# Token-major layout for the routing search's comparison tiles and list masks, fed by pairs of equal elements

## The chip, the cores and the metric

The kernel runs on one core of one Trainium2 chip. The metric is the device time of one execution in microseconds (us), the median of several runs. Engine names are those of the profile: PE is TensorE's matmuls, PEld its weight loads, DVE is VectorE, ACT is ScalarE, POOL is GpSimd, SP is the engine that issues most transfers.

## The reference

Three stages follow one another: a chunked attention, a two-layer MLP, and a mixture of 8 experts whose assignment is greedy over all (token, expert) scores. The change is in the third stage's assignment.

```python
def _moe2_ref(x, w_gate, w1, w2):          # x: 3072 x 512
    E = w_gate.shape[1]                    # 8 experts
    cap = N // E                           # 384 tokens each
    flat = (x @ w_gate).flatten()
    order = np.argsort(-flat)
    for idx in order:                      # best score first
        tok, e = idx // E, idx % E
        if assigned[tok] >= 0 or counts[e] >= cap:
            continue
        assigned[tok] = e
        counts[e] += 1
    ...
    for e in range(E):
        h = np.maximum(x[assigned == e] @ w1[e], 0.0)
        out[assigned == e] = h @ w2[e]
```

## The kernel before, in words

Attention and the MLP fill the first 670 us or so. Every large product there and in the experts is computed as three float32 products of high and low parts, and TensorE is what these stages run on. The experts follow. For each expert p the kernel finds which expert fills up next and with which tokens (`search`), makes the list of its 384 tokens (`tail`), gathers their rows, and runs the two products of that expert (`gemm1` at L610, `gemm2` at L633). Seven searches are run; the eighth expert takes what is left. A search for expert p+1 runs while the products of expert p are computed, so its small matmuls stand between large ones in TensorE's queue, and its vector work stands between the conversions of weights (L591, L593) on ACT and DVE.

A search looks for a score threshold, five or six bits of a 24-bit key at a time, in six levels (`LEVELS`). At each level `differ` forms the key's difference for the 24 tokens that each of the 128 partitions holds (`d`, 128 x 24), `compare` (L300) compares every one of them with 32 or 64 thresholds (`cm`, 24 x 32 = 768 or 24 x 64 = 1536 elements per partition, bfloat16), and `count` (L312) multiplies `cm` with the one-hot matrix `oh` of the tokens' best experts, so that each threshold's number of tokens per expert comes out. A matmul of `count` has 128 columns of `cm` as its weights: 32 thresholds of 4 tokens, in which case 6 matmuls with 32 moving columns make a level (four levels of a search), or 64 thresholds of 2 tokens, in which case 12 matmuls with 16 moving columns do (two levels). `less`, `threshold` and `base` (L318, L326, L329, L333) turn the counts into the next `d`. So a search is a chain that goes back and forth between DVE and PE.

For the list, `slots` computes each token's place (0 to 31, and 1 to 12), `places` and `parts` (L441, L448, L450) turn the two numbers into masks `A` and `rh`, and `tokens` (L459) multiplies them in 6 matmuls with 48 moving columns.

In all of these tiles the token column is innermost or nearly so: `cm` is stored as [group of tokens, threshold, token in the group], with 6 or 12 tokens in a group. A matmul takes one token of each group, so that the 128 weights lie 6 or 12 elements, 12 or 24 bytes, apart. `A` has the same layout with 6; the moving operand `rh` is also read in steps. The constants `i32`, `top` and `thr` are spread out over the tokens so that DVE reads whole rows of them.

The order of all instructions is written out when the program is built, by a planner (`Plan`) with fixed costs. Every engine then runs its own list in that order and waits for semaphores. Between the MLP's end and the first expert's products, TensorE runs a backlog of the MLP's second product (L1035) and then dummy matmuls (L663).

Of the kernel before, what the change touches and what calls it, by code (L numbers as in the profile page):

```python
# [170 lines left out]
UPPER = 4  # L171
PACK = 4


def routing_consts(nc, pool, jp, NTILE, E):
    V, G = nc.vector, nc.gpsimd
    c = {}

    def iota(name, cols, dt=FT, **kw):
        x = c[name] = pool.tile([128, cols], dt, name=name)  # L180
        G.iota(x, **({} if dt == I32 else dict(allow_small_or_imprecise_dtypes=True)), **kw)
        return x

    def fill(name, shape, dt, value):
        x = c[name] = pool.tile(shape, dt, name=name)
        V.memset(x, value)

    c["i32"] = pool.tile([128, 32, NTILE], F16, name="i32")
    G.iota(c["i32"], pattern=[[1, 32], [0, NTILE]], base=0, channel_multiplier=0, allow_small_or_imprecise_dtypes=True)
    top = pool.tile([128, 64, NTILE // 2], F16, name="top")  # L190
    G.iota(top, pattern=[[1, 64], [0, NTILE // 2]], base=1, channel_multiplier=0, allow_small_or_imprecise_dtypes=True)
    c["thr"] = []
    for n, (step, R) in enumerate(LEVELS):
        c["thr"].append(pool.tile([128, R, NTILE * R // 128], BF, name=f"thr{n}"))
        V.tensor_scalar(c["thr"][n], top[:, :R, :NTILE * R // 128], step, None, op0=OP.mult)
# [4 lines left out]
    iota("token", NTILE, F16, pattern=[[128, NTILE]], base=-HALF, channel_multiplier=1)  # L200
# [12 lines left out]


def phase2(tc, P, C, ident, L, x2d, we, out, ps_h, ps_o, ps_y, pools, lready, xready, open_pools, open_experts, room, roomy, before):
# [6 lines left out]
    nc = tc.nc  # L222
    NTILE, E = L.shape[1], L.shape[2]
# [52 lines left out]
    def differ(p, n):  # L276

        r = R[p]
        v = r["d"] = rt([128, NTILE], BF, "d")
        zero = C[0]["zero"]  # L280
        if n < UPPER:
            V.scalar_tensor_tensor(v, r["km"][:, n], r["pb"][:, 0:1] if n else 0.0, zero,
                                   op0=OP.subtract, op1=OP.subtract)
        else:
            if n == UPPER:
                r["no"] = rt([128, NTILE], FT, "no")
                V.scalar_tensor_tensor(r["no"], r["key"][2], r["pb"][:, 0:1], C[0]["far"],
                                       op0=OP.subtract, op1=OP.mult)
            V.scalar_tensor_tensor(v, r["km"][:, n], r["pb"][:, 1:2] if n > UPPER else 0.0, r["no"],
                                   op0=OP.subtract, op1=OP.subtract)  # L290
# [12 lines left out]

    def count(p, n):

        r = R[p]
        T, K, W = shape(n)
        r["pc"] = pools["ps_r"].tile([128, K * E], FT, name="pc")
        oh = r["oh"].rearrange("p (a b) e -> p a b e", b=W)
        cm = r["cm"].rearrange("p a t b -> p (a t) b")  # L310
        for j in range(W):
            nc.tensor.matmul(r["pc"], cm[:, :, j], oh[:, :, j, :], start=(j == 0), stop=(j == W - 1))  # L312

    def less(p, n, m):
        r = R[p]
# [110 lines left out]
    def slots(p):  # L426

        r = R[p]
        b = rt([128, NTILE], FT, "sb")
        a = rt([128, NTILE], I16, "sl")  # L430
        V.tensor_scalar(b, r["fx"][:, :NTILE], r["ps"], 32.0, op0=OP.add, op1=OP.add)
        V.tensor_tensor(a, b, r["F"], op=OP.mult)
        s = r["sl"] = rt([128, 2, NTILE], I16, "sp")
        V.tensor_scalar(s[:, 0], a, 31, None, op0=OP.bitwise_and)
        V.tensor_scalar(s[:, 1], a, 5, None, op0=OP.logical_shift_right)

    def places(p):
        c, r = C[0], R[p]
        W = NTILE // PACK
        r["A"] = rt([128, PACK, 32, W], F16, "A")  # L440
        V.tensor_tensor(r["A"], c["i32"][:, :, :W][:, None].to_broadcast([128, PACK, 32, W]),  # L441
                        r["sl"][:, 0].rearrange("p (a b) -> p a b", a=PACK)[:, :, None, :]
                        .to_broadcast([128, PACK, 32, W]), op=OP.is_equal)

    def parts(p):
        c, r = C[0], R[p]
        oc = rt([128, 12, NTILE], F16, "oc")
        V.tensor_tensor(oc, c["i32"][:, 1:13], r["sl"][:, None, 1].to_broadcast([128, 12, NTILE]), op=OP.is_equal)  # L448
        r["rh"] = rt([128, 12, NTILE], F16, "rh")
        V.tensor_tensor(r["rh"], oc, c["token"][:, None, :].to_broadcast([128, 12, NTILE]), op=OP.mult)  # L450

    def tokens(p):

        r = R[p]
        W = NTILE // PACK
        r["px"] = pools["ps_t"].tile([128, PACK, TT, 4], FT, name="pt")
        A, rh = r["A"], r["rh"].rearrange("p n (a b) -> p a n b", a=PACK)
# [105 lines left out]
    W, REG = {}, {}  # L563
# [97 lines left out]
    b, o = ps_o[0].take(), before  # L661
# [5 lines left out]
    for p in range(E):  # L667
# [7 lines left out]
        for f in range(NF + 2):  # L675
# [3 lines left out]
            s = NF * p + f - 2  # L679
# [9 lines left out]
def kernel(ctx, tc, q, k, v, w, w_gate_t, we, out):  # L689
# [513 lines left out]
    def expert_pools():  # L1203
# [67 lines left out]
```

## Time and profile before

| | |
|---|---|
| median of 3 runs | 1005.46 us (1004.71 to 1007.41) |
| time of the profiled execution | 1007.31 us |
| span of the profiled execution | 1005.3 us |
| PE busy | 983.8 us, 98% of the span |
| DVE busy | 768.5 us, 76% |
| ACT busy | 444.8 us, 44% |
| POOL busy | 131.6 us, 13% |
| mean granted TensorE clock | 0.996 of full speed |

Span is from the first to the last instruction; the profiled execution's own time is 2.0 us more. A matmul's recorded duration contains its way through the array, and records of neighbouring matmuls overlap, so what a matmul costs in a dense stretch is the distance from its start to the next one's start.

### The profile page before, as it was taken

The page shows a single profiled execution, that of the slowest core. Times are in us where ns is not written, and L with a number is a line of the kernel's source. Part 1 is how long each engine was busy: PE and PEld are TensorE (multiplying, and loading weights), DVE is VectorE, ACT ScalarE, POOL GpSimd, SP SyncE. Part 2 cuts the span into 40 slices and gives each one's busy share as a digit, 9 for nine tenths or more (in the row PEclk, how much of TensorE's full clock was granted, in tenths as well). Part 3 has the DMA queues.
Part 4 walks back from the last instruction along what each step waited for, and adds up shares of the span by engine and source line. Part 5 has one row for each costly group of instructions (what it writes and reads, how often), then busy time and mean ns, then how long its engine had stood idle before and what let it go on. Part 6 is the DMA issues. An engine that isn't in the chain of part 4 may idle for free.

```text
span 1005.3 us, 17330 instructions
## 1 busy us (share of the span) xinstructions
PE 983.8 (98%) x6068; PEld 856.7 (85%) x6068; DVE 768.5 (76%) x2573; ACT 444.8 (44%) x1187; POOL 131.6 (13%) x145
## 2 busy tenths in 40 slices
PE   8899999999999999999999999999999999999997
PEld 7778888888888888988888889778888888888996
DVE  6899798698698599699689494578887888875720
ACT  7777634444444443444444324023524334334521
POOL 0578521000000000000000000000121112111211
PEclk9999999999999999999999999999999999999999
DMA  7567510121011011110110000034542534526600
GB/s 260 196 212 236 191 58 29 31 74 44 29 61 58 30 61 50 38 62 30 58 62 11 1 1 31 12 119 133 174 162 96 199 113 141 170 71 202 227 32 32
DMA packets 36328, 95.50 MB, mean 95 GB/s; under 512 B 4369, under 2 KB 8465, under 8 KB 36113
## 3 DMA queue, kind: packets, MB, share of 16 engines
q1 hardware_dynamic: 32256, 81.54, 24.4%
q0 software_dynamic: 3840, 12.59, 3.7%
q8 instruction: 48, 0.79, 0.3%
q14 instruction: 40, 0.32, 0.1%
q10 hardware_dynamic: 144, 0.26, 0.1%
HBM read 81.79 MB, written 12.58 MB: 94 GB/s over the span
## 4 chain that ended last, share of the span: by engine, by line
PE 84%; DVE 7%; issue 4%; POOL 2%; ACT 1%; DMA 1%; POOLq 0%; DVEq 0%; ACTq 0%
PE po L1035 24%; PE ph L942 23%; PE ph L610 13%; PE po L633 12%; PE pa L824 3%; PE pa L894 2%; PE pc L312 2%; DVE junk L1065 2%; PE po L1090 2%; PE pa L867 2%; DVE wa L921 1%; DVE wp L919 1%; PE pt L479 1%; DVE wp L918 1%; DVE gs L951 1%
## 5 line engine op out<-in xcount | busy, mean ns | idle before, releaser
L1065 DVE CUSTOM_DVE_ANT_0 junk<-x,wgb 128x512 bf16<-128x512 f32 x296 | 207.5, 701 | 5.9 <-DMA wgb<-in_w_gate_t_dram 0.9
L950 ACT ACTIVATE gs<-ph 128x384 f32<-128x384 f32 x128 | 62.6, 489 | 196.9 <-PE ph L942 188.2
L1035 PE MATMUL po<-wouth,gh 128*128 128x512 f32 x336 | 136.4, 406 | 0.0
L1035 PE MATMUL po<-woutl,gh 128*128 128x512 f32 x336 | 133.7, 398 | 1.6 <-POOL woutl L926 1.6
L951 DVE TENSOR_TENSOR gs<-ph,gs 128x384 f32<-128x384 f32 x128 | 70.9, 554 | 82.2 <-ACT gs L950 81.8
L1035 PE MATMUL po<-wouth,gl 128*128 128x512 f32 x336 | 132.0, 395 | 0.7 <-POOL gl L953 0.7
L833 ACT ACTIVATE X<-X,st 96x128 f32<-96x128 f32 x248 | 96.9, 392 | 47.5 <-DVE st L828 47.3
L942 PE MATMUL ph<-x1h,winh 128*128 128x384 f32 x512 | 111.6, 339 | 0.4 <-DVE gs L951 0.4
L942 PE MATMUL ph<-x1h,winl 128*128 128x384 f32 x512 | 110.7, 337 | 0.2 <-POOL winl L926 0.2
L942 PE MATMUL ph<-x1l,winh 128*128 128x384 f32 x512 | 110.3, 336 | 0.0
L616 ACT ACTIVATE egh<-ph 128x384 fp32r<-128x384 f32 x64 | 31.4, 491 | 157.4 <-PE ph L610 148.0
L942 PEld LDWEIGHTS ph<-x1h,winh 128*128 128x128 f32 x512 | 91.6, 188 | 10.2 <-DVE gs L951 0.8
L942 PEld LDWEIGHTS ph<-x1h,winl 128*128 128x128 f32 x512 | 92.3, 188 | 1.4 <-POOL winl L926 0.5
L942 PEld LDWEIGHTS ph<-x1l,winh 128*128 128x128 f32 x512 | 91.1, 189 | 0.3
L1035 PEld LDWEIGHTS po<-wouth,gl 128*128 128x128 f32 x336 | 63.1, 188 | 15.4 <-POOL gl L953 1.9
L1035 PEld LDWEIGHTS po<-wouth,gh 128*128 128x128 f32 x336 | 63.1, 188 | 13.8
L1035 PEld LDWEIGHTS po<-woutl,gh 128*128 128x128 f32 x336 | 63.2, 188 | 13.1 <-POOL woutl L926 2.9
L952 ACT ACTIVATE gh<-gs 128x384 fp32r<-128x384 f32 x112 | 58.7, 524 | 34.4 <-DVE gs L951 34.0
L617 DVE SCALAR_TENSOR_TENSOR egl<-ph,egh 128x384 fp32r<-128x384 f32 x64 | 35.2, 551 | 45.1 <-ACT egh L616 45.0
L828 DVE CUSTOM_DVE_ANT_0 X<-pa,masks 96x128 f32<-96x128 f32 x232 | 56.3, 281 | 4.8 <-PE pa L824 4.8
L953 DVE TENSOR_TENSOR gl<-gs,gh 128x384 fp32r<-128x384 f32 x88 | 48.5, 551 | 10.7 <-ACT gh L952 10.6
L1150 POOL IOTA ij<- 128x128 int32 x1 | 0.2, 235 | 425.8 <-DVE L L1065 425.8
(245 smaller groups left out, 1938.9 us busy)
## 6 DMA issues: line engine op xcount, KB each, us to landing
west<-in_we_dram SPq DMA_DIRECT2D x56, 512.0 KB, 4.5
wst<-in_w_dram SPq DMA_DIRECT2D x32, 512.0 KB, 4.3
vt<-in_v_dram SPq DMA_DIRECT2D x30, 256.0 KB, 2.6
kt<-in_k_dram SPq DMA_DIRECT2D x30, 256.0 KB, 3.5
qt<-in_q_dram SPq DMA_DIRECT2D x31, 192.0 KB, 3.1
x2d<-x SPq DMA_DIRECT2D x21, 256.0 KB, 2.2
x<-in_we_dram SPq DMA_DIRECT2D x16, 256.0 KB, 2.8
wgb<-in_w_gate_t_dram SPq DMA_DIRECT2D x1, 2048.0 KB, 7.0
```

The lines of the kernel that those rows point to most:

```text
L610: nc.tensor.matmul(ph.t[:, :TB], w[a].t[:, k * 128:(k + 1) * 128], xs[x].t[:, k, :], start=(n == 0), stop=(n == 3 * KD - 1))
L617: b = P.op(("V", 0.47), lambda: V.scalar_tensor_tensor(gl.t, ph.t[:, :TB], 0.0, gh.t.bitcast(FT), op0=OP.max, op1=OP.subtract), [a], [ph, ...
L633: nc.tensor.matmul(ACC[p][i].t, l.t[:, 128 * i:128 * i + 128], w[a].t[:, 512:1024], start=(f == 0 and n == 0), stop=(f == NF - 1 and n == 2))
L828: V.tensor_tensor_reduce(out=X.t[:, h, :], in0=ps[h % 2].t[:QB, h // 2 * 128:h // 2 * 128 + 128], in1=masks[:, var, :], scale=-scale, scal ...
L833: S.activation(X.t[:, h, :], X.t[:, h, :], AF.Exp, bias=st.t[:, 0, h:h + 1], scale=-1.0, accum_out=st.t[:, 2, h:h + 1])
L942: nc.tensor.matmul(ph.t[:, :TB], win[wt][:, f, kk * 128:(kk + 1) * 128], xt.t[:, kk, :], start=(n == 0 and kk == 0), stop=(n == 2 and kk = ...
L950: o = P.op(("S", 0.37), lambda: S.activation(t.t, ph.t[:, :TB], AF.Copy, scale=0.01), [o], [ph, t], key=k)
L951: o = P.op(("V", 0.47), lambda: V.tensor_tensor(t.t, ph.t[:, :TB], t.t, op=OP.max), [o], [ph, t], key=k)
L952: x = P.op(("S", 0.42), lambda: S.activation(gh(), t.t, AF.Copy), [o, gd], [t, *gb], key=k)
L953: y = P.op({"V": 0.47} if j > 1 else {"V": 0.47, "G": 0.96} if j else {"G": 0.96}, lambda e=V if j > 1 else G: e.tensor_tensor(gl(), t.t, ...
L1035: nc.tensor.matmul(acc.t, lt()[:, sl], wout[wt][:, f, :], start=(f == 0 and n == 0), stop=(n == 2 and (f == NF - 1 or s == S6 - 1)), skip_ ...
L1065: V.tensor_tensor_reduce(out=pools["wgb"].tile([128, DM], BF, name="junk"), in0=x, in1=WGB[0][:, e, :], scale=1.0, scalar=0.0, op0=OP.mult ...
```

## The change

The token column becomes the outermost dimension. `cm` is [24 tokens, thresholds], `A` is [24, 32], `rh` is [24, 12]. The weights of each matmul in `count` and `tokens` are then 128 neighbouring elements, and the moving operands are neighbouring elements as well. For the comparison, a new helper `pairs` reads the row of thresholds two by two, and the token's value from a tile in which each value stands twice (`d` is 128 x 24 x 2, the list's places are 128 x 2 x 24 x 2, `token` is 128 x 48), so that the innermost dimension of all three operands has two neighbouring 16-bit elements. The constants shrink: `i32` from 768 elements per partition to 32, `top` from 768 to 64, `thr` from 192 or 768 to 32 or 64.

The planner's costs are not touched, and no instruction is added, removed or moved: PE, DVE, ACT, POOL and SP have 3532, 2492, 657, 141 and 290 rows in their written-out order before and after, and row by row they are the same instructions on the same tiles, but for the sizes of `d`, `sp`, `thr`, `i32`, `top` and `token`.

```diff
-    c["i32"] = pool.tile([128, 32, NTILE], F16, name="i32")
-    G.iota(c["i32"], pattern=[[1, 32], [0, NTILE]], base=0, channel_multiplier=0, allow_small_or_imprecise_dtypes=True)
-    top = pool.tile([128, 64, NTILE // 2], F16, name="top")
...
+    iota("i32", 32, F16, pattern=[[1, 32]], base=0, channel_multiplier=0)
+    top = iota("top", 64, F16, pattern=[[1, 64]], base=1, channel_multiplier=0)
...
-        c["thr"].append(pool.tile([128, R, NTILE * R // 128], BF, name=f"thr{n}"))
+        c["thr"].append(pool.tile([128, R], BF, name=f"thr{n}"))
...
     def differ(p, n):
-        v = r["d"] = rt([128, NTILE], BF, "d")
+        v = r["d"] = rt([128, NTILE, 2], BF, "d")
+        two = lambda x: x[:, :, None].to_broadcast([128, NTILE, 2])
...
+    def pairs(out, row, column, op):
+
+        n = row.shape[1] // 2
+        V.tensor_tensor(out.rearrange("p c (t u) -> p c t u", u=2),
+                        row.rearrange("p (t u) -> p t u", u=2)[:, None].to_broadcast([128, NTILE, n, 2]),
+                        column[:, :, None, :].to_broadcast([128, NTILE, n, 2]), op=op)
 
     def compare(p, n):
         c, r = C[0], R[p]
         T, K, W = shape(n)
-        cm = r["cm"] = rt([128, K, T, W], BF, f"cm{T}")
-        V.tensor_tensor(cm, c["thr"][n][:, None].to_broadcast([128, K, T, W]),
-                        r["d"].rearrange("p (a b) -> p a b", a=K)[:, :, None, :].to_broadcast([128, K, T, W]),
-                        op=OP.is_le)
+        cm = r["cm"] = rt([128, NTILE, T], BF, f"cm{T}")
+        pairs(cm, c["thr"][n], r["d"], OP.is_le)
 
     def count(p, n):
...
-        oh = r["oh"].rearrange("p (a b) e -> p a b e", b=W)
-        cm = r["cm"].rearrange("p a t b -> p (a t) b")
         for j in range(W):
-            nc.tensor.matmul(r["pc"], cm[:, :, j], oh[:, :, j, :], start=(j == 0), stop=(j == W - 1))
+            c = slice(j * K, j * K + K)
+            nc.tensor.matmul(r["pc"], r["cm"][:, c, :].rearrange("p a t -> p (a t)"),
+                             r["oh"][:, c, :].rearrange("p a e -> p (a e)"), start=(j == 0), stop=(j == W - 1))
...
-        s = r["sl"] = rt([128, 2, NTILE], I16, "sp")
+        s = r["sl"] = rt([128, 2, NTILE, 2], I16, "sp")
...
     def places(p):
-        r["A"] = rt([128, PACK, 32, W], F16, "A")
...
+        r["A"] = rt([128, NTILE, 32], F16, "A")
+        pairs(r["A"], c["i32"], r["sl"][:, 0], OP.is_equal)
 
     def parts(p):
-        oc = rt([128, 12, NTILE], F16, "oc")
...
+        oc = rt([128, NTILE, 12], F16, "oc")
+        pairs(oc, c["i32"][:, 1:13], r["sl"][:, 1], OP.is_equal)
...
     def tokens(p):
...
-            nc.tensor.matmul(r["px"], A[:, :, :, j].rearrange("p a m -> p (a m)"), rh[:, :, :, j],
-                             start=(j == 0), stop=(j == W - 1))
+            c = slice(j * PACK, j * PACK + PACK)
+            nc.tensor.matmul(r["px"], r["A"][:, c, :].rearrange("p a m -> p (a m)"),
+                             r["rh"][:, c, :].rearrange("p a n -> p (a n)"), start=(j == 0), stop=(j == W - 1))
```

## Rows read from the trace of the kernel before

**Rows 1.** The page: busy time and share of the span, TensorE.

```profile
PE 983.8 (98%) x6068; PEld 856.7 (85%) x6068; DVE 768.5 (76%) x2573; ACT 444.8 (44%) x1187; POOL 131.6 (13%) x145
```

**Rows 2.** Busy us by stretch: its length, then PE, PEld, DVE, ACT, POOL.

```profile
671.50:686.60 15.10, 11.80 (x104) 10.19 (x103) 11.83 (x37) 7.51 (x13) 3.56 (x3) 1.00 0.68 220
705.00:905.00 200.00, 200.00 (x1192) 169.06 (x1191) 167.40 (x610) 78.04 (x148) 33.73 (x44) 1.00 0.41 139
```

**Rows 3.** All that PE waited for from 620 us on: total us, times, longest.

```profile
PE pc L312 <- DVE cm L300: 1.5, 3, 0.7
PE ph L610 <- ACT xth L482: 1.1, 1, 1.1
PE pb L333 <- DVE fl L329: 1.0, 3, 0.6
PE ph L479 <- DMA xg<-x2d,idx: 0.8, 1, 0.8
```

**Rows 4.** Timeline, PE alone: three runs of small matmuls and what follows; start, duration.

```profile
637.77 0.45 PE L312 MATMUL pc<-oh,cm 128*128 128x32 bf16 x6
638.07 0.48 PE L1035 MATMUL po<-wouth,winl 128*128 128x512 f32 x1
...
653.95 0.87 PE L312 MATMUL pc<-oh,cm 128*128 128x16 bf16 x12
654.68 0.48 PE L1035 MATMUL po<-woutl,winh 128*128 128x512 f32 x1
...
665.15 0.72 PE L459 MATMUL pt<-rh,A 128*128 128x48 f16 x6
665.64 0.48 PE L1035 MATMUL po<-woutl,winh 128*128 128x512 f32 x1
```

**Rows 5.** The same, windows that end after the first two matmuls of a run.

```profile
637.77 0.27 PE L312 MATMUL pc<-oh,cm 128*128 128x32 bf16 x2
...
653.95 0.28 PE L312 MATMUL pc<-oh,cm 128*128 128x16 bf16 x2
```

**Rows 6.** The same: one matmul on packed bf16 weights; two with weights loaded before.

```profile
662.05 0.18 PE L424 MATMUL pt<-fx,tri 128*128 128x1 bf16 x1
662.09 0.47 PE L1035 MATMUL po<-wouth,winh 128*128 128x512 f32 x1
...
720.50 0.23 PE L312 MATMUL pc<-oh,cm 128*128 128x32 bf16 x2
```

**Rows 7.** Loads, matmuls by line, ns min/median/max; L312 in two runs, L424.

```profile
L312 PEld LDWEIGHTS <-cm x6: 125/144/148, 637.8 to 638.0; 128*128 128x128 bf16 x6
L312 PE MATMUL pc<-oh,cm x6: 197/198/219, 637.8 to 638.0; 128*128 128x32 bf16 x6
...
L312 PEld LDWEIGHTS <-cm x12: 140/166/168, 653.9 to 654.6; 128*128 128x128 bf16 x12
...
L424 PEld LDWEIGHTS <-tri x8: 95/96/98, 662.0 to 930.3; 128*128 128x128 bf16 x8
```

**Rows 8.** Groups by line and form, DVE: busy us, mean ns, idle before.

```profile
L593 DVE TENSOR_TENSOR wl<-west,wh 128x512 fp32r<-128x512 f32 x64 | 41.8, 683 | 0.0
...
L300 DVE TENSOR_TENSOR cm<-thr,d 128x768 bf16<-128x768 bf16 x28 | 15.5, 554 | 0.6
...
L300 DVE TENSOR_TENSOR cm<-thr,d 128x1536 bf16<-128x1536 bf16 x14 | 13.4, 955 | 0.3
...
L272 DVE TENSOR_TENSOR oh<-rev,be 128x192 bf16<-128x192 f32 x7 | 2.5, 358 | 0.2
```

**Rows 9.** Timeline where the routing constants are made.

```profile
598.99 0.93 POOL L189 IOTA i<- 128x768 f16 x1
...
599.87 1.08 POOL L191 IOTA top<- 128x768 f16 x1
...
601.00 0.15 POOL L181 IOTA token<- 128x24 f16 x1
...
603.19 0.96 PE L942 MATMUL ph<-x1h,winh 128*128 128x384 f32 x4 [0.35 <-DVE gs L951]
```

More of the change, by code (lines that the diff above doesn't have):

```diff
@@ L186, in fill @@
         V.memset(x, value)
-    c["i32"] = pool.tile([128, 32, NTILE], F16, name="i32")
-    G.iota(c["i32"], pattern=[[1, 32], [0, NTILE]], base=0, channel_multiplier=0, allow_small_or_imprecise_dtypes=True)
-    top = pool.tile([128, 64, NTILE // 2], F16, name="top")
-    G.iota(top, pattern=[[1, 64], [0, NTILE // 2]], base=1, channel_multiplier=0, allow_small_or_imprecise_dtypes=True)
+    iota("i32", 32, F16, pattern=[[1, 32]], base=0, channel_multiplier=0)
+    top = iota("top", 64, F16, pattern=[[1, 64]], base=1, channel_multiplier=0)
     c["thr"] = []
     for n, (step, R) in enumerate(LEVELS):
-        c["thr"].append(pool.tile([128, R, NTILE * R // 128], BF, name=f"thr{n}"))
-        V.tensor_scalar(c["thr"][n], top[:, :R, :NTILE * R // 128], step, None, op0=OP.mult)
+        c["thr"].append(pool.tile([128, R], BF, name=f"thr{n}"))
+        V.tensor_scalar(c["thr"][n], top[:, :R], step, None, op0=OP.mult)
     c["mask"] = pool.tile([128, len(LEVELS), NTILE], I32, name="mask")
@@ L199, in routing_consts @@
     iota("rev", E, pattern=[[-1, E]], base=E, channel_multiplier=0)
-    iota("token", NTILE, F16, pattern=[[128, NTILE]], base=-HALF, channel_multiplier=1)
+    iota("token", 2 * NTILE, F16, pattern=[[128, NTILE], [0, 2]], base=-HALF, channel_multiplier=1)
     fill("cap", [128, E], FT, float(NTILE * 128 // E))
@@ L278, in differ @@
         r = R[p]
-        v = r["d"] = rt([128, NTILE], BF, "d")
-        zero = C[0]["zero"]
+        v = r["d"] = rt([128, NTILE, 2], BF, "d")
+        two = lambda x: x[:, :, None].to_broadcast([128, NTILE, 2])
+        zero = two(C[0]["zero"])
         if n < UPPER:
-            V.scalar_tensor_tensor(v, r["km"][:, n], r["pb"][:, 0:1] if n else 0.0, zero,
+            V.scalar_tensor_tensor(v, two(r["km"][:, n]), r["pb"][:, 0:1] if n else 0.0, zero,
                                    op0=OP.subtract, op1=OP.subtract)
@@ L288, in differ @@
                                        op0=OP.subtract, op1=OP.mult)
-            V.scalar_tensor_tensor(v, r["km"][:, n], r["pb"][:, 1:2] if n > UPPER else 0.0, r["no"],
+            V.scalar_tensor_tensor(v, two(r["km"][:, n]), r["pb"][:, 1:2] if n > UPPER else 0.0, two(r["no"]),
                                    op0=OP.subtract, op1=OP.subtract)
@@ L432, in slots @@
         V.tensor_tensor(a, b, r["F"], op=OP.mult)
-        s = r["sl"] = rt([128, 2, NTILE], I16, "sp")
-        V.tensor_scalar(s[:, 0], a, 31, None, op0=OP.bitwise_and)
-        V.tensor_scalar(s[:, 1], a, 5, None, op0=OP.logical_shift_right)
+        s = r["sl"] = rt([128, 2, NTILE, 2], I16, "sp")
+        two = a[:, :, None].to_broadcast([128, NTILE, 2])
+        V.tensor_scalar(s[:, 0], two, 31, None, op0=OP.bitwise_and)
+        V.tensor_scalar(s[:, 1], two, 5, None, op0=OP.logical_shift_right)
     def places(p):
         c, r = C[0], R[p]
-        W = NTILE // PACK
-        r["A"] = rt([128, PACK, 32, W], F16, "A")
-        V.tensor_tensor(r["A"], c["i32"][:, :, :W][:, None].to_broadcast([128, PACK, 32, W]),
-                        r["sl"][:, 0].rearrange("p (a b) -> p a b", a=PACK)[:, :, None, :]
-                        .to_broadcast([128, PACK, 32, W]), op=OP.is_equal)
+        r["A"] = rt([128, NTILE, 32], F16, "A")
+        pairs(r["A"], c["i32"], r["sl"][:, 0], OP.is_equal)
     def parts(p):
         c, r = C[0], R[p]
-        oc = rt([128, 12, NTILE], F16, "oc")
-        V.tensor_tensor(oc, c["i32"][:, 1:13], r["sl"][:, None, 1].to_broadcast([128, 12, NTILE]), op=OP.is_equal)
-        r["rh"] = rt([128, 12, NTILE], F16, "rh")
-        V.tensor_tensor(r["rh"], oc, c["token"][:, None, :].to_broadcast([128, 12, NTILE]), op=OP.mult)
+        oc = rt([128, NTILE, 12], F16, "oc")
+        pairs(oc, c["i32"][:, 1:13], r["sl"][:, 1], OP.is_equal)
+        r["rh"] = rt([128, NTILE, 12], F16, "rh")
+        V.tensor_tensor(r["rh"].rearrange("p c (t u) -> p c t u", u=2), oc.rearrange("p c (t u) -> p c t u", u=2),
+                        c["token"].rearrange("p (c u) -> p c u", u=2)[:, :, None, :].to_broadcast([128, NTILE, 6, 2]),
+                        op=OP.mult)
     def tokens(p):
@@ L456, in tokens @@
         r["px"] = pools["ps_t"].tile([128, PACK, TT, 4], FT, name="pt")
-        A, rh = r["A"], r["rh"].rearrange("p n (a b) -> p a n b", a=PACK)
         for j in range(W):
-            nc.tensor.matmul(r["px"], A[:, :, :, j].rearrange("p a m -> p (a m)"), rh[:, :, :, j],
-                             start=(j == 0), stop=(j == W - 1))
+            c = slice(j * PACK, j * PACK + PACK)
+            nc.tensor.matmul(r["px"], r["A"][:, c, :].rearrange("p a m -> p (a m)"),
+                             r["rh"][:, c, :].rearrange("p a n -> p (a n)"), start=(j == 0), stop=(j == W - 1))
     def indices(p):
```

## The prediction

> **What bounds the kernel now.** I read the page first, for the engine that is never free: PE is busy for 98% of the span [rows 1]. Since that is an average, I then looked at stretches [rows 2]. From 705 to 905 us, where five of the seven searches lie between the experts' products, PE is busy for all of the 200.00 us and DVE for 167.40. In the start-up of the experts, 671.5 to 686.6 us, PE is busy for 11.80 of 15.10 us, dummies among them, and DVE for 11.83; there expert 0's weights and rows are awaited. The list of waits comes third: from 620 us to the end PE waited only 4.4 us in four rows [rows 3]. Behind 690 us, therefore, a microsecond taken out of PE's own queue is a microsecond of the span, and one taken out of DVE's is worth nothing until PE waits for it. So the question is what the small matmuls cost PE, and that is read from starts, not from recorded durations.
>
> **What a run of small matmuls costs now.** A run of 6 in `count` goes from 637.77 to the next large matmul at 638.07, 0.30 us; a run of 12 from 653.95 to 654.68, 0.73 us; a run of 6 in `tokens` from 665.15 to 665.64, 0.49 us [rows 4]. How the steps lie: two matmuls of the first run take 0.27 us together and one within a run lasts 0.198, so that the second starts 0.07 us after the first; in the run of 12 it is 0.28 less 0.20, 0.08 us [rows 5, 7]. The other steps are (0.30 - 0.07) / 5 = 0.046 us and (0.73 - 0.08) / 11 = 0.059 us. So 16 moving columns step more slowly than 32: it is not the moving operand that sets the step but the weights, which lie 24 bytes apart there and 12 here. The weight loads say the same: the first of a run, which waits behind nothing, takes 125 ns at 12 bytes and 140 ns at 24, but 95 to 98 ns for `tri`, whose 128 x 128 bf16 weights are packed [rows 7]. In `tokens` the weights lie 12 bytes apart too, and the mean step is 0.49 / 6 = 0.08 us; what is slower there is the moving operand, 48 elements that each lie apart from the next.
>
> **What it costs after.** No row shows packed weights in a run, so I bound the step. From below: where two sets of weights had been loaded ahead, the second matmul started 0.23 - 0.20 = 0.03 us after the first [rows 6]; nothing in these rows goes faster with 32 columns. From above: the step that the 12-byte weights have already, 0.046. Between: the lone matmul on `tri` gives way to the next after 0.04 us [rows 6], and the first step of a strided run is longer than its later ones by 0.02 (0.07 against 0.046, 0.08 against 0.059), because later loads overlap the matmul ahead. A lone packed matmul with 16 to 48 columns would take some 0.05, the later ones 0.02 less. I take 0.05 for the first and 0.03 for each other one, for all three kinds, since it is what both ways of reckoning give.
>
> - `count` with 32 thresholds: 0.05 + 5 x 0.03 = 0.20 in place of 0.30 us, 28 runs: 2.8 us.
> - `count` with 64: 0.05 + 11 x 0.03 = 0.38 in place of 0.73 us, 14 runs: 4.9 us.
> - `tokens`: 0.20 in place of 0.49 us, 8 runs: 2.3 us.
>
> Together 10.0 us of PE's queue. The large matmul behind each run still waits for its own weights; that part is not in these figures and stays.
>
> What of it is not on the path: in the start-up stretch three runs of the first kind and one of the second (0.65 us) lie where PE has time to spare; DVE's chain there does wait for them, so I take off 0.5. Search 0 lies beside the backlog. A shorter run lets the backlog end earlier, and with it the last row stores, on which the gathers wait; its counts come back earlier too, and with them the request for expert 0's weights. I count its share, 4 x 0.10 + 2 x 0.35 + 0.29 = 1.4 us, in full.
>
> **DVE.** `compare` has as many elements as before, all 16-bit. Going from 768 to 1536 elements costs 955 - 554 = 401 ns, 0.52 ns for each, while between 192 and 512 float32 elements it is (683 - 358) / 320 = 1.02 ns [rows 8]. So it handles two elements a step, and pairs of neighbours in all three operands should let it go on doing so. What is new is that one pair is read 16 or 32 times in a row. The one-hot row bears on that: `oh` reads each token's `be`, one 4-byte word, 8 times in a row, and its 358 ns fit the same fixed cost as the rest (358 - 192 x 1.02 = 162 ns, against 955 - 1536 x 0.52 = 156 for `compare`). I take 554 and 955 ns as unchanged. The other end is one element a step: 358 + 576 x 1.02 = 946 and 358 + 1344 x 1.02 = 1729 ns, 28 x 0.39 + 14 x 0.77 = 21.7 us more DVE work, 3.1 a search. `places` and `parts` follow `compare`; at the far end they add 0.4 and 0.3 us in each of 8 lists, in the same cover. `d` and the places' numbers have 24 elements more: 24 x 1.02 = 0.025 us in 42 + 16 instructions, 1.5 us. Their cover is DVE's 32.6 idle us of 200; without it they would cost those 1.5 us. I put the part in the start-up stretch, 4 or 5 of them, at 0.1 us.
>
> Here a rule of the Trainium skill speaks against the change. The Vector Engine (DVE) Microarchitecture Reference, in Measured stream behaviour on trn2, has a port at its full rate only while neighbours come in runs of at least two 4-byte words, and 1.73 ns in place of 1.054 where one source hops at every element. A pair of bf16 is one such word, and by that price `compare` would be longer by an estimated 384 x 0.68 = 0.26 us at 768 elements, 14.6 us over all. `oh` is read word by word too and shows none of it, so this trace disagrees, for words that are repeated.
>
> **The constants.** Two POOL instructions of 0.93 and 1.08 us shrink to about the 0.15 of the `token` one, and DVE, which waits for them, frees the buffer for which PE idles 0.35 us at 603.19 [rows 9]. DVE is then some 0.8 us ahead there, so I count 0.4 us.
>
> **The sum.** 10.0 - 0.5 - 0.1 + 0.4 = 9.8 us. The profiled execution took 1007.31 us for a span of 1005.3, so its like would take 997.5. It is the slow end of the three runs; taken off their median, 1005.46, it is 995.7, which I predict.
>
> **The rivals.** (a) Weights and moving columns do not overlap as well as assumed, and a packed step is 0.04 us, as for `tri` alone. Runs then take 0.25, 0.49 and 0.25 us and give 28 x 0.05 + 14 x 0.24 + 8 x 0.24 = 6.7 us, 6.4 after the small terms: 999.1. (b) A load and its matmul cannot be issued faster than the 12-byte step of 0.046. The first kind gains nothing, the second 0.73 - (0.07 + 11 x 0.046) = 0.15 us, `tokens` 0.19: 2.1 + 1.5 = 3.6 us, 3.4 after the small terms: 1002.1. That 0.03 has been seen only with loads that were early speaks for it. (c) The change does nothing for PE: the step's growth from 0.046 to 0.059 would come from the order of tokens or the two-row moving operand and not from the bytes between weights. Only the constants are left: 1005.1. The three load times against it are ordered as the distances are. The Trainium skill would have it so: TensorE: Matmul & The Clock Gate, Weight-path perf modes, gives the fast load 128 weights of a 16-bit type as its condition and its pattern as "packed or strided", without a price for the stride; the 125 and 140 against 96 ns of this trace disagree. (d) Slower: `compare` falls to one element a step, DVE gets 21.7 us more, and in the steady stretch has 167.40 + 15.5 us of work in some 193, 95%, while every egl and weight conversion waits behind it. If all of it came to the path it would be 1005.46 + 21.7 - 9.8 = 1017.4; it decides the sign once more than 9.8 of the 21.7 us, 45%, reach PE. The idle share of DVE speaks against so much, `oh` against the fall itself.
>
> **How the numbers follow.** Forecast, a gain of 8 to 13 us: 0.62. (a) 0.17, (b) 0.08, (c) 0.08, (d) 0.05. The fast end is a step of 0.02, which gives 28 x 0.06 + 14 x 0.11 + 8 x 0.06 = 3.7 us more, 992.0. The slow end takes in (a) and most of (b), 1001.5, and leaves out some 0.15 above. About 0.3%, 3 us, is what a measurement can tell from no change. Faster are the forecast, (a) and 0.05 of (b): 0.84; within it the rest of (b) and (c): 0.11; slower 0.05.
>
> **What would show it.** Right: in the timeline a run of 12 in `count` of about 0.38 us to the next large matmul, a run of 6 in `count` and one in `tokens` of about 0.20; first weight loads of 95 to 98 ns on `cm` and `A`; `cm` groups still at some 554 and 955 ns; PE without new waits from 705 to 905 us; the wait at 603 us gone. Wrong: `cm` near 950 and 1730 ns with PE waiting for it, or for the conversions at L593 and L617; runs that keep their length with short loads, which would be (b); or shorter runs with a span that does not follow, which would mean that the backlog, the start-up's transfers or the order on DVE set the end there.

## The result and the profile after

| | before | after |
|---|---|---|
| median of 5 runs on the same chip | 1005.39 us (1004.71 to 1007.41) | 995.56 us (994.27 to 995.88) |
| profiled execution, time and span | 1007.31, 1005.3 us | 995.56, 993.8 us |

The medians differ by 9.8 us. The ratio of the two kernels' times is 0.9898, which is 10.3 us, with an interval of 0.9888 to 0.9908, 9.2 to 11.3 us: the change makes the kernel about 1% faster.

The page of the changed kernel, its first lines: busy time, share of the span and instructions, as in [rows 1].

```profile
span 993.8 us, 17323 instructions
...
PE 971.8 (98%) x6068; PEld 844.4 (85%) x6068; DVE 768.8 (77%) x2573; ACT 444.9 (45%) x1187; POOL 130.7 (13%) x145
```

PE's busy time fell by 12.0 us, from 983.8, and PEld's by 12.3, while DVE's stayed where it was (768.5). All of the gain is PE's, and PE is still busy for 98% of what is left. The same three runs of small matmuls as in [rows 4], timeline of PE alone, start and duration:

```profile
646.22 0.32 PE L315 MATMUL pc<-oh,cm 128*128 128x32 bf16 x6
646.38 0.48 PE L1039 MATMUL po<-wouth,x1l 128*128 128x512 f32 x1
...
649.57 0.46 PE L315 MATMUL pc<-oh,cm 128*128 128x16 bf16 x12
649.88 0.48 PE L1039 MATMUL po<-wouth,winl 128*128 128x512 f32 x1
...
663.60 0.32 PE L463 MATMUL pt<-rh,A 128*128 128x48 f16 x6
663.76 0.47 PE L1039 MATMUL po<-woutl,winh 128*128 128x512 f32 x1
```

From the start of a run to the start of the next large matmul it is now 0.16, 0.31 and 0.16 us, where it was 0.30, 0.73 and 0.49. The 0.32 and 0.46 us that stand beside `x6` and `x12` are recorded durations with the way through the array in them; read alone they would say that the run of 12 takes half as long again as it does. With a first step of 0.04 us the others are (0.164 - 0.04) / 5 = 0.025 us in the first and third kind and (0.316 - 0.04) / 11 = 0.025 in the second, 0.164 and 0.316 being medians over all runs of a kind. Over all runs (medians of before: 0.302, 0.743, 0.497) PE's queue became shorter by 28 x 0.138 + 14 x 0.427 + 8 x 0.333 = 3.86 + 5.98 + 2.66 = 12.5 us.

Weight loads and matmuls by line, ns min/median/max, as in [rows 7]:

```profile
L315 PEld LDWEIGHTS <-cm x336: 95/96/102, 637.6 to 885.9; 128*128 128x128 bf16 x168
L315 PE MATMUL pc<-oh,cm x336: 169/176/193, 637.6 to 885.9; 128*128 128x32 bf16 x84, 128*128 128x16 bf16 x84
L463 PEld LDWEIGHTS <-A x48: 95/96/101, 663.6 to 922.7; 128*128 128x128 f16 x48
```

All 336 + 48 loads now take what `tri` took, 95 to 102 ns. Over all their loads, `count` and `tokens` took 124 to 182 ns before.

DVE, groups by line and form, as in [rows 8]:

```profile
L298 DVE TENSOR_TENSOR cm<-thr,d 128x768 bf16<-128x768 bf16 x28 | 15.6, 556 | 0.6
L298 DVE TENSOR_TENSOR cm<-thr,d 128x1536 bf16<-128x1536 bf16 x14 | 13.4, 956 | 0.3
...
L281 DVE SCALAR_TENSOR_TENSOR d<-km,pb,zero 128x48 bf16<-128x48 int32 x21 | 5.7, 272 | 3.8 <-PE pb L337 3.1 <-PE ph L614 0.2
```

The comparison with pairs takes 556 and 956 ns, in place of 554 and 955. The Trainium skill's rule that was weighed against this, on single 4-byte words (Vector Engine (DVE) Microarchitecture Reference, Measured stream behaviour on trn2), has no hold on a word that is read 16 or 32 times in a row: by its price it would have been some 260 ns more at 768 elements.

Everything that PE waited for from 620 us on, in us, times, longest, as in [rows 3]:

```profile
PE pb L337 <- DVE fl L333: 1.6, 4, 0.7
PE ph L614 <- ACT xth L486: 1.1, 1, 1.1
PE pc L315 <- DVE cm L298: 0.8, 1, 0.8
PE pc L315 <- issue: 0.6, 1, 0.6
PE ph L483 <- DMA xg<-x2d,idx: 0.3, 1, 0.3
PE pb L337 <- issue: 0.3, 1, 0.3
```

The sum is 4.7 us, against 4.4. That is not all that PE waits more, since a matmul's record still runs while the next one is held up, and the list begins a wait at the record's end. The windows show the beginning of it, start-up and steady stretch as in [rows 2]:

```profile
669.40:683.05 13.65, 10.93 (x105) 9.45 (x103) 11.70 (x37) 7.21 (x13) 3.09 (x3) 1.00 0.75 243
700.00:893.00 193.00, 192.28 (x1197) 160.54 (x1196) 168.49 (x608) 79.30 (x150) 34.05 (x44) 1.00 0.43 147
```

PE is no longer busy for every microsecond of the steady stretch (192.28 of 193.00), and DVE has 87% of it in place of 84%. Starts show the rest: from a `gemm1` matmul to a `base` matmul (L333 before, L337 after) that follows it, 15 of them between the first products of experts 1 and 6, it was 0.270 us in the mean and is 0.325. Ten of the 15 are at 0.271 as before; the others grew, the longest to 0.646, 0.498 and 0.425.

Where the constants are made, the wait of 0.35 us is gone, and the two long POOL instructions of [rows 9] take 0.16 and 0.18 us:

```profile
599.36 0.16 POOL L181 IOTA i<- 128x32 f16 x1
599.48 0.18 POOL L181 IOTA top<- 128x64 f16 x1
599.70 0.40 POOL L181 IOTA token<- 128x48 f16 x1
...
603.10 0.87 PE L946 MATMUL ph<-x1h,winh 128*128 128x384 f32 x4
```

The gain by stage, from instruction starts in two profiled executions of each kernel (the second ones are the runs `e7_before_again` and `e8_after_again` below):

| us | before | before, again | after | after, again |
|---|---|---|---|---|
| start to last `gemm1` matmul of the MLP | 629.90 | 630.42 | 629.90 | 627.87 |
| from there to expert 0's first product | 56.8 | 55.3 | 53.2 | 53.1 |
| from there to the end | 318.7 | 318.6 | 310.7 | 311.3 |
| within that, expert 1 to expert 6 | 203.2 | 203.2 | 196.8 | 196.8 |

The first row is nearly the same instructions and scatters by up to 2.5 us from one execution to the next. Some of that is the clock: in the two first profiles the granted clock of TensorE was 0.91 in the mean of 620 to 640 us, around the edge between the first two rows, with PE busy throughout, and in the two repeats 1.00. The steady stretch, expert 1 to expert 6, repeats to 0.1 us. It became 6.4 us shorter. The 16 runs of 6, 9 of 12 and 5 of `tokens` in it became shorter by 16 x 0.138 + 9 x 0.427 + 5 x 0.333 = 7.7 us. So 1.3 us of the gain there came back. The order of PE's instructions is the same, so each start-to-start distance can be set against its own: 1.1 us of the 1.3 stand in front of `base`, 0.2 in front of `count`.

From expert 0's first product to the end it is the same in a larger measure. The runs there, 20 of 6, 11 of 12 and 7 of `tokens`, became 9.5 us shorter, summed run by run, and 7.9 and 7.3 us were gained, 7.6 in the mean. Of what came back, 1.4 us stand in front of `base` in both pairs of executions, and 0.2 and 0.9 in front of `count`. Ahead of that product the runs became 2.7 us shorter and 2.9 were gained.

### The profile page after: what moved, and what is told of

It reads as the page before. It is cut to its first block, busy times and chain, and to the rows that moved or that the text cites. A ratio compares the mean times of both kernels' runs of the same rounds, so it can differ in the third digit from the quotient of the medians.

```text
span 993.8 us, 17323 instructions
## 1 busy us (share of the span) xinstructions
PE 971.8 (98%) x6068; PEld 844.4 (85%) x6068; DVE 768.8 (77%) x2573; ACT 444.9 (45%) x1187; POOL 130.7 (13%) x145
## 4 chain that ended last, share of the span: by engine, by line
PE 83%; DVE 8%; issue 4%; ACT 1%; DMA 1%; POOL 1%; POOLq 0%; DVEq 0%; ACTq 0%; SPq 0%
PE po L1039 24%; PE ph L946 24%; PE ph L614 13%; PE po L637 11%; PE pa L828 3%; PE pa L898 2%; PE pa L871 2%; PE po L1094 2%; DVE junk L1069 2%; DVE wp L923 1%; DVE wa L925 1%; DMA wst<-in_w_dram 1%; PE pt L483 1%; DVE wp L922 1%; PE pc L315 1%
## 5 line engine op out<-in xcount | busy, mean ns | idle before, releaser
L1039 PEld LDWEIGHTS po<-wouth,gh 128*128 128x128 f32 x336 | 63.1, 188 | 13.7
```

The source lines that it names most:

```text
L1039: nc.tensor.matmul(acc.t, lt()[:, sl], wout[wt][:, f, :], start=(f == 0 and n == 0), stop=(n == 2 and (f == NF - 1 or s == S6 - 1)), skip_ ...
```

## The experiments

All are variants of the changed kernel or of the one before, timed beside the kernel before; a ratio is to that.

**The two halves.** `e1_count_only` has the new comparison and count with the old lists; `e2_lists_only` has the old comparison with the new lists.

```diff
-        r["A"] = rt([128, NTILE, 32], F16, "A")
-        pairs(r["A"], c["i32"], r["sl"][:, 0], OP.is_equal)
+        r["A"] = rt([128, PACK, 32, W], F16, "A")
+        V.tensor_tensor(r["A"], c["i32"][:, :, :W][:, None].to_broadcast([128, PACK, 32, W]),
...
```

Against the changed kernel that is the edit of e1, and this is the edit of e2:

```diff
-        cm = r["cm"] = rt([128, NTILE, T], BF, f"cm{T}")
-        pairs(cm, c["thr"][n], r["d"], OP.is_le)
+        cm = r["cm"] = rt([128, K, T, W], BF, f"cm{T}")
+        V.tensor_tensor(cm, c["thr"][n][:, None].to_broadcast([128, K, T, W]),
...
```

> Only the comparison tiles of the search are token-major and packed; the list masks and their constant are as before. Theory (the time is the length of the runs in PE's queue): 28 runs go from 0.30 to 0.164 us and 14 from 0.74 to 0.316, 9.8 of the 12.4 us by which the whole change shortens PE's queue, so 9.8/12.4 of the 9.8 us gained: a gain of 7.0 to 8.5 us, 997 to 998.5. Rival (a good part of the gain is won in the start-up through the list, whose matmuls stand in front of the first gathers): a gain of 5 us or less, over 1000.

> Only the list masks are token-major and packed; comparison tiles as before. Theory: 8 runs go from 0.50 to 0.164 us, 2.7 us of PE's queue, a gain of 2.0 to 2.7 us, 1002.7 to 1003.4. Rival (the list's runs matter more than their length, through the gathers that follow): a gain of 4 us or more, under 1001.5.

Measured: e1 997.8 us, ratio 0.992 (0.9906 to 0.9935), a gain of 8.0 us. e2 1001.65 us, 0.996 (0.9947 to 0.9972), 4.0 us, which is above what the theory gave and at the edge of what the rival gave. From expert 0's first product to the end e2 takes 316.3 us, 2.3 less than before, in the range of the theory. The other 1.7 us would lie ahead of that product; its profiled execution (1003.31 us, the slowest of e2's five) does not have them, so whether the lists gain there or the first stages scattered is not shown. In the same stretch e1 takes 313.0, 5.6 less. Together that is 7.9, against the change's 7.6: the two halves add up, and neither hides the other.

**Pairs taken away.** `e3_no_pairs` keeps the new layout and its packed weights, but lets the comparison read one value of `d` for the whole row of thresholds.

```diff
-        v = r["d"] = rt([128, NTILE, 2], BF, "d")
+        v = r["d"] = rt([128, NTILE], BF, "d")
...
-        pairs(cm, c["thr"][n], r["d"], OP.is_le)
+        V.tensor_tensor(cm, c["thr"][n][:, None].to_broadcast([128, NTILE, T]),
+                        r["d"][:, :, None].to_broadcast([128, NTILE, T]), op=OP.is_le)
```

> As the change, but the comparison reads each token's value with an innermost step of 0 instead of from pairs. Both views expect cm groups near 946 and 1729 ns in place of 556 and 956, 21.7 us more DVE work. Theory (PE bounds the stages behind 690 us, DVE has 12 to 13% to spare there): PE's runs stay at 0.164 and 0.316 us and most of it is hidden; 1 to 6 us over the change, 996.5 to 1001.5. Rival (DVE is close enough to the bound that the pairs are what the gain hangs on): over 8 us more, 1003.5 or above.

Measured: 1007.39 us, ratio 1.0015 (1.0006 to 1.0024). That is 11.8 us over the changed kernel, more than the whole gain; the rival was right and my theory fell. DVE groups, PE's waits, and the steady window of [rows 2], in e3:

```profile
L305 DVE TENSOR_TENSOR cm<-thr,d 128x768 bf16<-128x768 bf16 x28 | 26.8, 957 | 0.6
L305 DVE TENSOR_TENSOR cm<-thr,d 128x1536 bf16<-128x1536 bf16 x14 | 24.6, 1756 | 0.3
...
PE pc L315 <- DVE cm L305: 8.8, 16, 1.1
PE pb L337 <- DVE fl L333: 2.6, 8, 0.6
...
705.00:905.00 200.00, 193.09 (x1178) 159.16 (x1177) 180.68 (x601) 77.67 (x147) 34.21 (x44) 1.00 0.42 137
```

Without pairs the comparison does one element at a time: 957 and 1756 ns, 22.4 us more DVE work in all. The matmuls are as short as in the changed kernel. DVE is busy for 180.68 of 200 us, so 10% of its time is idle, and yet 53% of the 22.4 us reached the end, because PE now stands in front of `count`: from the matmul ahead to the `count` behind it the median distance grew from 0.238 to 0.352 us for 32 thresholds and from 0.230 to 0.852 for 64, in sum 28 x 0.114 + 14 x 0.622 = 11.9 us; distance by distance the sum is 11.9 us too. That is as much as the whole difference. In front of `base` another 1.3 us are added, and about as much is won back in the scatter of the stages ahead. The Trainium skill has the same fall (Vector Engine (DVE) Microarchitecture Reference, Performance modes): an operation with two 16-bit sources ran one element at a time where one source read a single element 16 times. The 957 ns agree.

**Count twice.** `e4_count_twice` issues the packed matmuls of each level two times, which adds 28 x 6 x 0.025 + 14 x 12 x 0.025 = 8.4 us to PE's queue and nothing to DVE's.

```diff
-        for j in range(W):
+        for _ in range(2):
+            for j in range(W):
```

> As the change, but every run of count is done twice over (the second starts the sums anew, so the result is the same): 336 matmuls more at 25 ns, 8.4 us more in PE's queue and nothing anywhere else. Theory (a microsecond of PE's queue is a microsecond of the time, but in the start-up): 6.5 to 8.5 us over the change, 1002 to 1004. Rival (the runs' length works mainly through the latency of the search, or PE has hidden slack): under 4 us over the change.

Measured: 1005.12 us, ratio 0.999 (0.9981 to 0.9999), some 9.2 us over the changed kernel, by the two intervals about 8 to 10.5. The median lies over the theory's range, and the rival is out: what these runs take is paid for. The first run of 12 and what follows it, timeline of PE in e4:

```profile
635.67 0.47 PE L316 MATMUL pc<-oh,cm 128*128 128x32 bf16 x12
635.99 0.48 PE L1040 MATMUL po<-wouth,winl 128*128 128x512 f32 x1
```

Twelve matmuls of 32 columns take 0.32 us, as long as twelve of 16 do: the columns do not set the step. By stage the extra time is 6.0 us from expert 0's first product on, where the runs became 6.3 us longer; there the price is nearly whole. In the start-up it is more than 3 us (17.5 us from the end of the backlog to the first product, where it is 13.7 and 14.4 in the two executions of the changed kernel), although the runs there became only 0.8 us longer. That is not the runs' doing, as the windows of the two halves of e4's start-up show:

```profile
668.83:678.00 9.17, 7.08 (x81) 6.18 (x80) 7.42 (x24) 4.25 (x7) 3.16 (x3) 1.00 0.71 221
678.00:686.35 8.35, 6.76 (x56) 6.22 (x56) 5.27 (x15) 3.53 (x7) 0.00 (x0) 0.62 0.59 184
```

The granted clock was 1.00 in the first half, in which PE was busy for 7.08 of 9.17 us, and 0.62 in the mean of the second, part of it at the lower of its two levels (1.2 in place of 2.4 GHz). In the changed kernel's start-up it was 1.00. So the 3 us of this profile say nothing of what a longer run costs in the start-up.

**A ladder of distances.** `e5_ladder` groups the tokens of a level by 2, 4 or 6, so that the weights lie 4, 8 and 12 bytes apart; the two levels of 16 moving columns get 8 and 12.

```diff
+GROUP = [2, 2, 2, 2, 4, 6]
...
-        cm = r["cm"] = rt([128, NTILE, T], BF, f"cm{T}")
-        pairs(cm, c["thr"][n], r["d"], OP.is_le)
+        g = GROUP[n]
+        cm = r["cm"] = rt([128, NTILE // g, T, g], BF, f"cm{T}{g}")
...
+            c, b = slice(j // g * K, j // g * K + K), j % g
+            nc.tensor.matmul(r["pc"], r["cm"][:, c, :, b].rearrange("p a t -> p (a t)"), oh[:, c, b, :],
```

> As the change, but the comparison tiles hold tokens in groups of 2 (the four levels of 32 thresholds), 4 and 6 (the two levels of 64), so that weights lie 4, 8 and 12 bytes apart; the moving columns stay at 32 and 16, and DVE reads pairs of tokens, not doubled ones. Theory (the distance between weights sets the step): the first weight load of a run and the step grow with the distance: near 96 ns and 25 to 30 ns at 4 bytes, between at 8, and at 12 bytes 125 ns and 46 to 47 ns although the moving columns are 16. Rival (16 moving columns of two token rows, not the distance, made the step 59): at 12 bytes with 16 columns the step is 59 again, and 25 at 12 bytes with 32 would have been due to something else.

Measured: 997.61 us, ratio 0.9922 (0.9905 to 0.9939). Timeline of PE in e5, a run of each kind with what follows it, and the weight loads of single runs:

```profile
635.86 0.32 PE L320 MATMUL pc<-oh,cm 128*128 128x32 bf16 x6
636.02 0.48 PE L1044 MATMUL po<-wouth,winl 128*128 128x512 f32 x1
...
647.77 0.57 PE L320 MATMUL pc<-oh,cm 128*128 128x16 bf16 x12
648.19 0.48 PE L1044 MATMUL po<-wouth,winl 128*128 128x512 f32 x1
...
651.13 0.73 PE L320 MATMUL pc<-oh,cm 128*128 128x16 bf16 x12
651.71 0.47 PE L1044 MATMUL po<-woutl,winh 128*128 128x512 f32 x1
...
L320 PEld LDWEIGHTS <-cm x12: 111/118/131, 647.8 to 648.1; 128*128 128x128 bf16 x12
...
L320 PEld LDWEIGHTS <-cm x12: 125/144/145, 651.1 to 651.6; 128*128 128x128 bf16 x12
```

The same 16 columns take 0.42 us at 8 bytes, 0.58 at 12, and 0.73 at 24 in the kernel before, but 0.31 packed. The shortest load of a run, which waits behind nothing, is 111, 125 and 140 ns. The rival, that 16 columns are slow in themselves, is out, and the step grows with the grouping. One thing was not varied by itself: with the group the rows of `oh`, the moving operand, move apart too, 32, 64, 96 and 192 bytes for groups of 2, 4, 6 and 12. For the weights speak the loads, which read nothing of `oh` and grow from 96 to 140 ns, and that four rows of `oh` at 96 bytes step as fast (0.046 us, the runs of 6 before) as two rows at 96 bytes do here (0.047). So that the distance between weights sets the step is well supported, but not isolated.

**The moving operand.** `e6_rh_strided` has packed weights in `tokens`, but moving columns 48 bytes apart.

```diff
-        r["rh"] = rt([128, NTILE, 12], F16, "rh")
+        r["rh"] = rt([128, 12, NTILE], F16, "rh")
...
-                             r["rh"][:, c, :].rearrange("p a n -> p (a n)"), start=(j == 0), stop=(j == W - 1))
+                             r["rh"][:, :, c].rearrange("p n a -> p a n"), start=(j == 0), stop=(j == W - 1))
```

> As the change, but rh keeps its old layout, so that in the list's product the weights A are packed and the 48 moving elements lie 48 bytes apart each; two constants are added for it. Theory (the moving operand set the step of that run): weight loads at 96 ns, the step still 85 to 92 ns, the run near 0.49 us. Rival (the weights set it): the step at 25 to 30 ns, the run near 0.17 us.

Measured: 996.62 us, ratio 0.9901 (0.9885 to 0.9918). The total cannot tell 2 us from nothing; the timeline can:

```profile
661.57 0.68 PE L464 MATMUL pt<-rh,A 128*128 128x48 f16 x6
662.03 0.48 PE L1040 MATMUL po<-woutl,winh 128*128 128x512 f32 x1
```

The run takes 0.46 us, with weights as packed as in the changed kernel, where it takes 0.16. So in `tokens` the moving operand was the slow one, as the prediction had it from the mean step of 0.08 us. From expert 0's first product on e6 takes 313.1 us, some 2 more than the changed kernel, for 7 x 0.30 = 2.1 us of longer runs there. (The edit also makes DVE's comparison for `oc`, from which `rh` is made, slower, 452 in place of 326 ns; that does not touch the length of a run.)

**Each kernel again.** `e7_before_again` and `e8_after_again` are the two kernels unchanged, to see what a difference between two profiles is worth.

> The kernel before, profiled once more, to see how much of the 13.65 against 15.18 us between the end of the backlog and the first expert product is scatter. Theory (the start-up waits for transfers and scatters by a microsecond or more from one execution to the next): a start-up between 13.5 and 15.2 us. Rival (the change shortens the start-up by 1.5 us): 15.0 to 15.3 us again.

> The changed kernel, profiled once more, for the same question. Theory (scatter): the start-up anywhere between 13.5 and 15 us. Rival (the change shortens it): 13.5 to 13.8 us again. The runs of small matmuls are as in the first profile.

Measured: 1006.26 and 994.1 us. The start-up took 14.7 us in e7 and 14.4 in e8, both in the range of scatter and outside that of the rival: these two executions show no gain in the start-up that stands clear of its scatter. The stages are in the table above: 0.1 us of scatter in the steady stretch, up to 0.7 in the start-up and from expert 0's first product to the end, and up to 2 us ahead of the MLP's last `gemm1` matmul.

**Two by two.** `e9_group2` is the ladder with `GROUP = [2] * 6`: weights 4 bytes apart, `thr` spread over two tokens, and `d` with its 24 elements as before the change. It tells whether the 21 to 27 ns that the doubled `d` costs (272 in place of 251 ns in the largest group) are on the path.

> As the change, but the comparison tile holds tokens two by two in all six levels (weights 4 bytes apart), so that DVE reads pairs of different tokens and d stays at 24 elements; the order of instructions is the same. Theory (weights 4 bytes apart step like packed ones, and where PE now waits for a search's DVE chain, each of the 25 ns that doubling d added is on the path): runs of 0.164 and 0.316 us, d back at 184 and 250 ns, 0.5 to 1.5 us under the change, 994 to 995.5. Rival (the doubled d is hidden): within 0.3 us of it; or 4 bytes cost something with 16 moving columns: runs of 12 over 0.35 us.

Measured: 994.82 us, ratio 0.9897 (0.9884 to 0.9911), 310.5 us from expert 0's first product on. The median lies in the theory's range, but the kernel before was faster beside it too (1004.79 in place of 1005.39 us), and the ratio is the changed kernel's but for 0.0001. The steps decide: distance by distance, the time in front of `base` behind expert 0's first product differs by 0.06 us between e9 and the changed kernel. So the doubled `d` is hidden; my theory that it was behind the waits at `base` fell, and the same wait stands in e9:

```profile
PE pb L342 <- DVE fl L338: 1.6, 4, 0.7
```

It shows too that 4 bytes between weights cost nothing: pairs of neighbouring tokens do as well as pairs of equal elements.

**The planner told the new lengths.** The order is planned with costs of the old runs. `e10_group2_costs` is e9, `e11_change_costs` the changed kernel, with the measured lengths (and 0.03 us more for `differ` in e11); `e12_no_pairs_costs` is e3 with the comparison's real length.

```diff
-            o = small((0.047 if n < UPPER else 0.06) * W, lambda n=n: count(p, n), [o], late=late)
+            o = small(0.0265 * W, lambda n=n: count(p, n), [o], late=late)
...
-        o = small(0.53, lambda: tokens(p), ts, late=late)
+        o = small(0.165, lambda: tokens(p), ts, late=late)
```

That is the edit of e10 and e11, and this is the edit of e12, against e3:

```diff
-            o = P.op(("V", 0.08 + K * T * W / 1920), lambda n=n: compare(p, n), [o])
+            o = P.op(("V", 0.08 + K * T * W / 960), lambda n=n: compare(p, n), [o])
```

> As the kernel with tokens two by two, and the planner is told the measured lengths of the runs (0.0265 us a matmul in count, 0.165 us for tokens), which moves large matmuls between the small ones. Theory (a part of the gain came back as PE waiting for DVE at base and count, because the order still allows for longer runs): those waits shrink and another 0.5 to 1.5 us are gained, 992.5 to 994.5. Rival (the waits are DVE's own chain, which no order shortens, or a new order opens other waits): no gain, or a loss of up to 3 us.

> As the change, with the planner told the measured lengths of the runs and 0.03 us more for the doubled d. Theory: 0.5 to 1.5 us under the change, 994 to 995.5. Rival: no gain, or a loss of up to 3 us.

> As the version without pairs, whose slow comparison cost 11.8 us over the change, but the planner is told the comparison's true rate (one element a step). Theory (that cost is the written-out order: count stands in PE's queue where the fast comparison would be done, so PE waits although DVE has time): with more large matmuls ahead of each count at least half comes back, 1001.5 or less. Rival (DVE's load is the bound): it stays within 3 us, 1004.5 or more.

Measured: e10 999.03 us, ratio 0.9937 (0.9922 to 0.9952), some 4 us slower than e9. e11 1000.19 us, 0.9948 (0.9935 to 0.9962), some 5 slower than the changed kernel. e12 1011.72 us, 1.0067 (1.0055 to 1.0079), some 5 slower than e3. All three orders are worse: e10 and e11 by more than the 3 us that the rival allowed, and e12 on the rival's side of 1004.5 us but not within 3 us of e3. PE's waits in e11 and then in e12:

```profile
PE pb L337 <- DVE fl L333: 4.2, 5, 1.4
```

```profile
PE pb L337 <- DVE fl L333: 7.2, 11, 1.5
PE pc L315 <- DVE cm L305: 6.0, 8, 2.7
PE pt L483 <- issue: 2.5, 2, 1.3
```

In e11 the wait for `fl` grew from 1.6 to 4.2 us; in e12 less is waited for at `count` than in e3 (6.0 in place of 8.8), and more at `base` (7.2 in place of 2.6), and in front of the transposes of the gathered rows into `pt` (L483) there are 4.9 us of waits that e3 does not have; the longest of them are shown. Part of e12's loss is the clock, as two windows of e12 show:

```profile
840.00:850.00 10.00, 7.23 (x45) 5.16 (x45) 8.98 (x24) 5.66 (x12) 3.81 (x5) 1.00 0.82 281
850.00:860.00 10.00, 6.87 (x38) 6.32 (x38) 8.54 (x19) 3.10 (x6) 0.00 (x0) 0.66 0.01 4
```

In the first, PE was busy for 7.23 of 10 us at a granted clock of 1.00; in the second the granted clock was 0.66 in the mean, and an estimated 10 x 0.34 x 0.69 = 2.3 us of this profile were lost by it, 0.69 being PE's busy share. How much of the loss is the clock's in the other executions is not known; their mean clocks are 0.991 to 0.994, this one's is 0.996. In e10 and e11 the executions with a mean of 0.998 (996.75 to 998.83 us, and 997.82) are in the mean still 3 to 4 us slower than those of e9 and the changed kernel at 0.998, so there it is mainly the order. A planner that knows the lengths better did not give a better order; its other fixed costs are of the same kind, and which of them the old figures happened to make up for was not tried. Nor is it shown that no order could hide e3's longer comparison.

## Why the prediction was right

It gave 995.7 us, and the median is 995.56. The mechanism was right; that the number was met to 0.1 us is luck, as the steps show:

- **PE's queue sets the time behind 690 us.** Right: e4 added 8.4 us to it and the time grew by some 9.2; behind expert 0's first product, where the clock is all but undisturbed, 6.3 us added cost 6.0.
- **The distance between weights sets a run's step, and in `tokens` the moving operand.** Right as far as it is shown: for `tokens` e6 shows it; for the weights e5 supports it, with the rows of `oh` moving apart at the same time. Rival (c), no effect on PE, is out by the result itself.
- **Packed steps of 0.05, then 0.03 us, and runs of 0.20, 0.38 and 0.20.** Right in kind and mis-sized: 0.04, then 0.025, and 0.16, 0.31 and 0.16. The term of 10.0 us measured 12.5. The lower bound of 0.03, from two preloaded matmuls [rows 6], was not a bound: it is 0.028 in the trace, and packed steps are 0.025. The 0.039 of the lone matmul on `tri` is what the first step became. Rivals (a) and (b), 0.04 and 0.046 us, are out.
- **0.5 us taken off for the start-up.** That step was probably wrong, but it is not shown. From the MLP's last `gemm1` matmul to expert 0's first product 2.9 us were gained (means 56.1 and 53.1), where search 0's 1.4 and the start-up's 0.65 less 0.5 had been allowed for; the runs there became 2.7 us shorter, 0.8 of it in the start-up. In both pairs of executions the distances in front of `count` and `base` did not grow in this stretch (together -0.04 and +0.02 us), so nothing was given back there. But the stretch itself scatters by up to 1.4 us, and the chain that ends last goes through a transfer in the start-up in the profiles of the kernel before, e4, e7, e8 and e9, if not in the first one of the changed kernel.
- **All the rest of PE's gain reaches the end.** Not quite: behind expert 0's first product 9.5 us of shorter runs gave 7.6, so that 1.9 us came back (1.3 of them in the steady stretch), most of it at `base`, where PE now waits for DVE. The prediction named no such term, and its sign of being right, no new waits of PE from 705 to 905 us, did not appear.
- **`compare` unchanged, doubled `d` hidden.** Right: 556 and 956 ns, and e9.
- **The constants, 0.4 us.** The wait of 0.35 us is gone; more cannot be read from it among the scatter of the first 630 us.
- **Rival (d), a comparison at one element a step, priced at 946 and 1729 ns and 21.7 us of DVE.** Its price was right, e3 measured 957, 1756 and 22.4. The argument against its reaching the path was wrong. The idle share of DVE was said to speak against 45%, and 53% came through with DVE idle for 10% of the stretch. What kept the gain was the fall that did not take place, not cover on DVE.

So two errors, 2.5 us too little for the runs and 1.9 too much for what of them reaches the end, nearly cancelled. The stages behind the MLP's last `gemm1` matmul gained 2.9 + 7.6 = 10.5 us by the profiles, the ratio says 10.3, and the medians differ by 9.8. What is left between these, and the 0.4 us for the constants, is lost in the scatter of the first 630 us.

## What to carry to other kernels

Where many small matmuls stand in a full TensorE queue, read their cost as the distance from the run's first start to the next instruction's start, and look at how far apart the weights and the moving elements lie: packing both took 46 to 67% off these runs. Pay for the layout on the engine that writes it by keeping the innermost two elements of every operand real neighbours; here that alone decided between 1% faster and slightly slower. And do not take an engine's idle share as cover for a step in a chain that goes back and forth between two engines: ask who waits at that step, since with 10% of DVE idle more than half of its added work reached the end.

## What the runs showed of the hardware

- Runs of a 128 x 128 16-bit weight load and a matmul with 16, 32 or 48 packed moving columns step by 25 ns when the weights lie 2 or 4 bytes apart, by 33 ns at 8 bytes (0.42 us for 12), by 47 at 12 bytes (0.58 for 12) and by 59 to 60 at 24 bytes (0.743 for 12). The first load takes 95 to 96, 96, 111, 125 and 140 ns. (In these runs the rows of the moving operand move apart with the weights, see e5.) The Trainium skill gives the read pattern of the fast weight load as "packed or strided" (TensorE: Matmul & The Clock Gate, Weight-path perf modes); in this case's traces a strided read has the price above.
- 48 moving fp16 elements 48 bytes apart make the step 86 ns with packed weights (e6, 0.46 us for 6).
- An iota of 48 elements that writes each value twice took 0.40 us by its record, against 0.15 for the 24 elements before [rows 9], and 0.18 for 64 elements without repetition.
- The comparison for `oc` starts 2 bytes into the row of constants, reads it in pairs, and took 326 ns for 288 elements, against 300 when it read whole rows; one element at a time (e6) it took 452. The product for `rh`, of the same size and in pairs without the offset, took 308 before and after; that the 26 ns are the offset's was not tried apart.

```profile
L298 DVE TENSOR_TENSOR oc<-i,sp 128x288 f16<-128x288 f16 x8 | 2.6, 326 | 0.0
```
